# The tail of a block-transform 7x7 convolution: 128-column matrices, another split of the last evictions and of the last writes

## The chip, the cores and the metric

The kernel runs on one core of one Trainium2 chip. The metric is device time in microseconds of one execution. Five engines work side by side, each with its own queue of instructions: TensorE (PE; its weight loads are shown as PEld), VectorE (DVE), ScalarE (ACT), GpSimd (POOL) and SyncE (SP), which only issues DMAs and waits. DMAs may be issued from SP, POOL or ACT.

## The reference

A circular convolution of a 224 x 224 x 96 image with 7 x 7 x 96 x 96 weights, written as a product of two-dimensional real Fourier transforms:

```python
def reference(x, w):
    B, H, W, C = x.shape          # 1, 224, 224, 96
    K = w.shape[0]                # 7
    wp = jnp.pad(w, ((0, H - K), (0, W - K), (0, 0), (0, 0)))
    Xf = rfft2(x.astype(float32), axes=(1, 2))
    Wf = rfft2(wp.astype(float32), axes=(0, 1))
    Yf = jnp.einsum('bhwi,hwio->bhwo', Xf, Wf)
    return irfft2(Yf, s=(H, W), axes=(1, 2)).astype(bfloat16)
```

Image, weights and result are bfloat16.

## The kernel before

The image's rows are cut into NJ = 8 blocks of B = 28 rows, each with 6 rows of overlap, and every block is carried along the rows into a short real transform of length 32 (plus two extra points), 17 "slots" of two real parts each. Along the columns there is no transform: seven taps, with even and odd pixels treated apart. The columns are handled in NT = 7 tiles of 32 pixels. For each tile and slot, `b_round` does the tap products on TensorE (stationary: the transformed pixels, 128 columns; moving: 96 transformed weights of `WF`), and VectorE and GpSimd make the sums into `yf`. For tiles 0 to 5 the sums are written to a scratch tensor in DRAM, read back in another layout (`tt`) and turned into output rows with the matrix `G` (`c_jobs`), while the next tile's tap products run.

The last tile, TL = 6, does not go through DRAM. Its sums stay in SBUF (`YA` for the first SA = 13 slots, `YB` for the other four), VectorE transposes them in 32 x 32 blocks into `TA` and `TB` (`turn_a`, `turn_b`), and the inverse transform uses other matrices, `GY`: one for `TA` (`GA`) and four for `TB` (`GB`). `GY` is built on GpSimd by five copies from `GX`, which small DMAs fill from `G` (`g_parts`, L661 to L672), during the middle tiles; `GX` is set to zero first (L824). Each matrix has 4 * B = 112 columns, one for each of the 28 rows in each of 4 column quarters.

The tail is the code from L879 on. After `turn_b` and the remaining `c_jobs`, 16 units (j, h) are worked off, j the block of rows and h the half of the pixels:

- `first(j, h)` takes a PSUM bank and does one matmul with `GA`, 384 moving elements.
- `second(j, h, ...)` adds four matmuls with `GB`, 96 moving elements each, and then calls `tail_evac`, which copies the bank to SBUF as bfloat16.
- Eight firsts run ahead. The seconds follow in order, and from the fifth second to the twelfth each is followed by one more first (8 banks of PSUM, LF = 4), so first number 8 + n needs the bank of eviction n.
- After each odd unit, both halves of block j are in `yo`, and one DMA writes 28 rows x 4 quarters x 768 elements to the output (168 KB).

`tail_evac` counts calls in `tail[0]`, which is set to 2 just before, and gives odd counts to VectorE and even ones to ScalarE. The writes go by block: even j from SP (`DE`), odd j from GpSimd (`GE`), the last, j = 7, from ScalarE (`SE`). Instructions of one engine are held in program order by the `_Ordered` wrapper, so all instructions carry L86 in the profile, the line of its helper, and are told apart by their tiles. `evac`, the function for evictions before the tail, shares them out by a running estimate of load, and passes them to `tail_evac` when `tail[0]` is not zero.

Of the kernel before, what the change touches and what calls it, by code (L numbers as in the profile page):

```python
# [8 lines left out]
BF16 = mybir.dt.bfloat16  # L9
# [5 lines left out]
B = 28  # L15
# [5 lines left out]
NJ = 8  # L21
# [13 lines left out]
SA = 13  # L35
NB4 = 4
YMAX = 3
YBUF = 4
JGB = ((0, 3), (3, 6), (6, 9), (9, 12), (12, 15), (15, 17))
LAG = 4  # L40
# [13 lines left out]
def kernel(  # L54
# [38 lines left out]
    VE, SE, GE, TE, DE = (_Ordered(e) for e in (nc.vector, nc.scalar, nc.gpsimd, nc.tensor, nc.sync))  # L93
# [9 lines left out]
    def bank():  # L103
        return pools["psb"].tile([128, 512], F32, name="pb")

    load = {"v": 0.0, "a": 0.0}
    tail = [0]
# [7 lines left out]
        return r  # L115

    def evac(out_ap, in_ap, n):
        if tail[0]:
            return tail_evac(out_ap, in_ap, n)
        cv, ca = 180 + 1.0 * n, 160 + 0.85 * n  # L120
        if load["v"] + cv <= load["a"] + ca:
            load["v"] += cv
            return VE.tensor_copy(out=out_ap, in_=in_ap)
        load["a"] += ca
        return SE.copy(out=out_ap, in_=in_ap)

    def tail_evac(out_ap, in_ap, n):
        tail[0] += 1
        return VE.tensor_copy(out=out_ap, in_=in_ap) if tail[0] % 2 else SE.copy(out=out_ap, in_=in_ap)

    def dma(out_ap, in_ap):
        return DE.dma_start(out=out_ap, in_=in_ap)
# [258 lines left out]
    def new_xf(t, s0=0, s1=NS):  # L391
        xf = xf_bufs[t % 2]
        xf_tiles[t] = xf
        if t > 0:
            prev = xf_tiles[t - 1]
            for ph in range(2):
                o, i = (v[0:C, ph, :, s0:s1, p:p + HALO, :].rearrange("c r s w j -> c r s (w j)") for v, p in ((xf, 0), (prev, TW)))
                apart(("A", t), ("halo", s0), SE.copy(out=o, in_=i))
                load["a"] += 160 + 0.85 * 2 * (s1 - s0) * HALO * NJ
        return xf  # L400
# [34 lines left out]
    def then_load(f, t, jg):  # L435
        def g():
            f()
            if t < NT:
                load_x(t, jg)
        return g  # L440
# [11 lines left out]
    def f_jobs(t, part):  # L452
        s0, s1 = SH2[part], SH2[part + 1]
        n = 2 * (s1 - s0) * JG
        nr = -(-TW * n // 512)
        e = [-(-TW * i // nr) for i in range(nr + 1)]
        fv = Fm[:, :, s0:s1].rearrange("p r s j -> p r (s j)")

        def mk_(jg, a, b, ph):
            def f():  # L460
                pa = bank()
                for k in range(b - a):
                    i = 2 * (a + k) + ph
                    TE.matmul(pa[:, k * n:(k + 1) * n], lhsT=xbuf(t, jg)[:, i * C:i * C + 128], rhs=fv, start=True, stop=True)
                xo = xf_tiles[t][0:C, ph, :, s0:s1, HALO + a:HALO + b, jg * JG:(jg + 1) * JG]
                pi = pa[0:C, 0:(b - a) * n].rearrange("c (w r s j) -> c r s w j", r=2, s=s1 - s0, w=b - a)
                return apart(("A", t), (a, jg, ph, part), evac(xo, pi, (b - a) * n))
            return f
        return [[mk_(jg, a, b, ph) for a, b in zip(e[:-1], e[1:]) for ph in range(2)] for jg in range(2)]
# [40 lines left out]
    def b_round(t, s, mid, end, ydve=False, planes=()):  # L510
# [11 lines left out]
        else:  # L522
            for (y0, y1) in YGRP:
                if s == y0:
                    yf_cur[t] = (yf_pool.tile([128, YMAX, 2, 2, C], BF16, name="yf"), y0, y1)
            yf, y0, y1 = yf_cur[t]
# [134 lines left out]
    def g_parts():  # L661
        for q in range(4):
            dma(GX[q * SR:q * SR + 2 * SA, 0, q * B:q * B + B], G[0:2 * SA, 0:B])
            yield
        for q in range(4):
            for b in range(NB4):
                r = q * SR + b * SRB
                dma(GX[r:r + SRB, 1 + b, q * B:q * B + B], G[2 * SA:2 * NS, 0:B])
                yield
        for k in range(NB4 + 1):  # L670
            GE.tensor_copy(out=GY[:, k].rearrange("p (m q) -> p q m", q=4), in_=GX[:, k].rearrange("p (q m) -> p q m", q=4))
            yield  # L672

    yo_free = [J_bufs[2][0:4 * B, i * PXC * C:(i + 1) * PXC * C] for i in range(2)]
# [58 lines left out]
    def queue_c(t):  # L733
        pend.extend((t, *k) for k in LT)
        pump()
# [20 lines left out]
    stmp_cm.__exit__(None, None, None)  # L756
    yf_pool = ctx.enter_context(tc.tile_pool(name="yf", bufs=YBUF))
    tv_pool = ctx.enter_context(tc.tile_pool(name="tv", bufs=2))
# [12 lines left out]
    def fills(qs, k):  # L771
        def f():
            for q in qs:
                pace(q, k)
        return f
# [3 lines left out]
    def add(a, b, jobs):  # L779
        qs.append([a, b, jobs, len(jobs)])  # L780
# [14 lines left out]
    for r in range(NS + LAG):  # L795
        if r == 0:
            add(0, 4, fj[1][1] + fj[2][1])
        for p in range(3):
            if r == (1, 3, 5)[p]:
                new_xf(1, SH2[p], SH2[p + 1])  # L800
                fj = f_jobs(1, p)
                if p == 2:
                    for jg in range(2):
                        fj[jg][-1] = then_load(fj[jg][-1], 2, jg)
                add(2 * r + 1, 2 * r + (5, 5, 4)[p], fj[0] + fj[1])
        for p in range(3):
            if r == SH2[p + 1] + 1 - (p == 2):
                new_xf(2, SH2[p], SH2[p + 1])
                fj = f_jobs(2, p)
                if p == 2:  # L810
                    for jg in range(2):
                        fj[jg][-1] = then_load(fj[jg][-1], 3, jg)
                add(2 * r, 2 * r + (8, 7, 5)[p], fj[0] + fj[1])
        if r == PGRP[-2][1] + 1:
            assert not any(q[2] for q in qs[:len(PGRP) - 1])
            wtmp_cm.__exit__(None, None, None)
            t_pool = ctx.enter_context(tc.tile_pool(name="tt", bufs=NTT, side="right"))
            t2_pool = ctx.enter_context(tc.tile_pool(name="tt2", bufs=1, side="right"))
            yo_pool = ctx.enter_context(tc.tile_pool(name="yo", bufs=2, side="right"))
            g_pool = ctx.enter_context(tc.tile_pool(name="gp", bufs=1, side="right"))  # L820
            GX = g_pool.tile([128, 1 + NB4, 4 * B], BF16, name="GX")
            GY = g_pool.tile([128, 1 + NB4, 4 * B], BF16, name="GY")
            GA, GB = GY[:, 0], GY[:, 1:]
            GE.memset(GX[:], 0.0)  # L824
        if r == NS + 3:
            queue_c(0)
        for t in range(2):
            s = r - LAG * t
            if not 0 <= s < NS:
                continue  # L830
            now = bursts.pop((r, t), ())
            now = jit(*now) if now else ()
            both = LAG <= r < NS
            b_round(t, s, fills(qs, 2 * r + (t if both else 0)), fills(qs, 2 * r + (t if both else 1)), False, now)
    assert not bursts and nburst == 2 * len(JGB)
    if NP2:
# [3 lines left out]
        pools["ps"], pools["psb"] = (c.__enter__() for c in ps_cms)  # L840
    cj = c_jobs(0)
    gp = g_parts()
    for t in range(2, NT):
        if t == TL:
# [35 lines left out]
    load["v"] = 2 * BIAS + load["a"]  # L880
    for f in cj:
        f()
    tail[0] = 2
    assert not pend
    if NP2:
        for c in reversed(ps_cms):
# [2 lines left out]
    NC = 2 * 2 * C  # L889
    MO = 4 * B  # L890

    def first(j, h):
        pc = bank()[0:MO, 0:NC]
        TE.matmul(pc.rearrange("p (w g e) -> p w g e", w=2, e=4), lhsT=GA, rhs=TA[:, 2 * h:2 * h + 2, j], start=True, stop=False)
        return pc

    def second(j, h, pc, yo):
        po = pc.rearrange("p (w g b e) -> p b w g e", w=2, b=NB4, e=4)
        for b in range(NB4):
            TE.matmul(po[:, b], lhsT=GB[:, b], rhs=TB[:, 2 * h:2 * h + 2, j], start=False, stop=b == NB4 - 1)  # L900
        tail_evac(yo[0:MO, (j % 2) * 2 * NC + h * NC:(j % 2) * 2 * NC + (h + 1) * NC], pc, NC)
    order = [(j, h) for j in range(NJ) for h in range(2)]
    warm(WARM0)
    live = {k: first(*k) for k in order[:8]}
    LF = 4
    for i, (j, h) in enumerate(order):
        if i % 4 == 0:
            yo = t_pool.tile([128, TW // 2, 2 * C], BF16, name="tt").rearrange("p w e -> p (w e)")
        second(j, h, live[(j, h)], yo)
        k = i + 8 - LF  # L910
        if 8 <= k < len(order):
            live[order[k]] = first(*order[k])
        if i % 2 == 1:
            w0 = TL * 2 * TW
            eng = SE if j == NJ - 1 else GE if j % 2 else DE
            eng.dma_start(out=out[0, j * B:(j + 1) * B, w0:w0 + 2 * TW, :].rearrange("m (q w) c -> m q (w c)", q=4), in_=yo[0:MO, (j % 2) * 2 * NC:(j % 2 + 1) * 2 * NC])
    if not NP2:
        ps0_cm.__exit__(None, None, None)
# [30 lines left out]
```

## Time and profile before

| what | us |
|---|---|
| time, median of 3 runs | 265.87 (265.08 to 266.10) |
| the profiled execution, time | 266.41 |
| its span, first to last instruction | 264.7 |
| granted TensorE clock, mean | 0.993 |
| tail: 16 firsts and 64 seconds on TensorE | 252.78 to 259.04 |
| tail: evictions, VectorE | 8 of 0.55 each |
| tail: evictions, ScalarE | 8 of 0.48 each |
| tail: writes from SP, POOL, ACT | 4, 3, 1 |

The page gives busy times of each engine and, in its part 4, the chain of work that ended last, followed back from the end. The timeline lists instructions by start; adjacent ones of one engine and one kind are merged into a row with a count. "SPq" and "ACTq" are the engines' queues issuing a DMA; the duration there is that of issuing, not of the transfer. In rows by form, two numbers after the bar are busy microseconds and the mean of one in nanoseconds, and after the second bar stands the idle time before them with what ended it. The last columns of a row of windows are the granted clock, the DMA engines' busy share and GB/s. Times in all views count from the first instruction.

### The profile page before, as it was taken

How to read it: one execution, taken by the hardware profiler on the slowest of the kernel's cores; microseconds unless marked ns; L12 is line 12 of the kernel's file. 1: busy time of each engine (PE TensorE's matmuls, PEld its weight loads, DVE VectorE, ACT ScalarE, POOL GpSimd, SP SyncE). 2: the span in 40 equal slices, each digit the busy share in tenths (PEclk: the TensorE clock that was granted, in tenths of full speed). 3: DMA queues.
4: the chain of work that ended last, by engine and by line, in shares of the span. 5: the costliest groups of instructions: out<-in, count | busy, mean ns of one | idle time of the engine just before them, and what ended most of it. 6: DMA issues, size and time to landing. Idle time of an engine off the chain costs nothing.

```text
span 264.7 us, 12207 instructions
## 1 busy us (share of the span) xinstructions
PE 252.5 (95%) x5160; PEld 234.3 (89%) x5160; DVE 215.8 (82%) x459; ACT 198.6 (75%) x500; POOL 101.5 (38%) x166
## 2 busy tenths in 40 slices
PE   8799998999999999999999999999999999999981
PEld 3569898999999999998999998999999999999861
DVE  5729799898978979977888788777978889899981
ACT  5529997659795566898988869989798886666652
POOL 7781033345355553234123332543143222424420
PEclk9999999999999999999999999999999999999997
DMA  6766210451111299896979449597959753585135
GB/s 162 182 192 152 73 51 2 154 159 47 50 47 47 85 254 208 239 268 180 290 226 244 150 108 315 180 258 185 325 193 206 209 186 125 145 169 155 55 111 175
DMA packets 41416, 43.44 MB, mean 164 GB/s; under 512 B 30836, under 2 KB 33104, under 8 KB 41362
## 3 DMA queue, kind: packets, MB, share of 16 engines
q1 hardware_dynamic: 41044, 41.98, 56.6%
q8 instruction: 40, 0.66, 1.1%
q0 software_dynamic: 192, 0.52, 0.7%
q10 hardware_dynamic: 126, 0.17, 0.2%
q14 instruction: 14, 0.11, 0.1%
HBM read 22.09 MB, written 19.66 MB: 158 GB/s over the span
## 4 chain that ended last, share of the span: by engine, by line
PE 82%; ACT 5%; DVE 4%; issue 3%; DMA 3%; POOL 1%; SPq 1%; DVEq 0%; ACTq 0%
PE pb L86 82%; ACT WF L86 3%; DMA WF<-in_x_dram 3%; DVE WF L86 1%; ACT xf L86 1%; POOL yf L86 1%; DVE J L86 1%; DVE u L86 1%; DVE xf L86 1%; SPq L86 1%; DVE yf L86 0%; ACT tt L86 0%; DVE v L86 0%; ACT tt__676 L86 0%; ACT tt__2951 L86 0%
## 5 line engine op out<-in xcount | busy, mean ns | idle before, releaser
L86 PE MATMUL pb<-WF,J 96*128 96x96 bf16 x2821 | 162.6, 206 | 0.5 <-DVE WF L86 0.3
L86 PEld LDWEIGHTS <-J 96*128 96x128 bf16 x2821 | 137.9, 98 | 8.7 <-DVE u L86 1.5
L86 POOL TENSOR_TENSOR yf<-v,u 128x384 bf16<-128x384 f32 x70 | 69.1, 1001 | 129.5 <-issue 69.2
L86 ACT CAST xf<-pb 96x408 bf16<-96x408 f32 (+3 forms) x143 | 67.2, 487 | 10.3 <-PE pb L86 8.5
L86 PE MATMUL pb<-WF,xf 96*128 96x96 bf16 x952 | 60.2, 206 | 1.1 <-ACT xf L86 0.5
L86 DVE TENSOR_TENSOR J<-xf 96x1824 bf16<-96x1824 bf16 (+1 forms) x84 | 57.5, 724 | 0.1
L86 PEld LDWEIGHTS <-xf 96*128 96x128 bf16 x952 | 47.3, 98 | 1.9 <-issue 0.9
L86 PE MATMUL pb<-Fm,xn 118*128 118x136 bf16 (+3 forms) x640 | 45.5, 199 | 0.9 <-DVE u L86 0.8
L86 ACT CAST WF<-pb 96x480 bf16<-96x480 f32 (+1 forms) x59 | 29.0, 573 | 5.0 <-PE pb L86 5.0
L86 PE MATMUL pb<-tt,Gm 102*84 102x384 bf16 (+1 forms) x132 | 32.1, 326 | 0.0
L86 PEld LDWEIGHTS <-xn 118*128 118x128 bf16 x640 | 30.5, 97 | 1.2 <-issue 1.2
L86 ACT CAST yo<-pb 84x384 bf16<-84x384 f32 (+1 forms) x66 | 28.2, 484 | 2.9 <-PE pb L86 2.6
L86 ACT CAST J<-pb 84x384 bf16<-84x384 f32 (+1 forms) x65 | 28.0, 484 | 2.8 <-PE pb L86 2.8
L86 DVE TENSOR_TENSOR J<-J 96x912 bf16<-96x912 bf16 (+2 forms) x42 | 22.8, 542 | 0.0
L86 PE MATMUL pb<-wq 98*128 98x120 bf16 (+1 forms) x288 | 21.2, 225 | 0.0
L86 PEld LDWEIGHTS <-wq 98*128 98x128 bf16 x288 | 19.4, 148 | 0.2
L86 PE MATMUL pb<-wu 128*128 128x512 bf16 x43 | 11.8, 435 | 1.1 <-DVE ct L86 1.1
L86 DVE TENSOR_TENSOR yf<-v,u 128x384 bf16<-128x384 f32 x20 | 11.3, 567 | 0.7
L86 PEld LDWEIGHTS <-Gm 102*84 102x84 bf16 (+1 forms) x132 | 11.1, 117 | 0.8
L86 DVE CAST WF<-pb 96x480 bf16<-96x480 f32 (+1 forms) x13 | 7.5, 610 | 5.4 <-PE pb L86 5.2
L86 POOL TENSOR_TENSOR xn<-v,u 128x384 bf16<-128x384 f32 x8 | 7.2, 926 | 11.8 <-DVE v L86 11.8
L86 ACT COPY xf<-xf 96x816 bf16<-96x816 bf16 (+3 forms) x20 | 11.2, 621 | 0.0
(404 smaller groups left out, 254.3 us busy)
## 6 DMA issues: line engine op xcount, KB each, us to landing
scr<-yf SPq DMA_DIRECT2D x30, 288.0 KB
xn<-in_x_dram SPq DMA_DIRECT2D x12, 672.0 KB
tt<-scr SPq DMA_DIRECT2D x24, 336.0 KB
out_dram<-yo SPq DMA_DIRECT2D x12, 252.0 KB
out_dram<-J SPq DMA_DIRECT2D x12, 252.0 KB
tt<-scr SPq DMA_DIRECT2D x6, 288.0 KB
WF<-in_x_dram SPq DMA_DIRECT2D x2, 672.0 KB
scr<-yf SPq DMA_DIRECT2D x6, 192.0 KB
```

What stands on the lines that cost most here:

```text
L86: r = fn(*a, **k)
```

## The change

Three edits in the tail. `GY` gets 128 columns for each matrix instead of 112, with zeros in the last 16, and the PSUM outputs of `first` and `second` have 128 rows, of which the first 112 are evicted. `tail_evac` counts from 0 and gives VectorE the seven calls of `TAILV`, ScalarE the other nine. Blocks 1 and 3 are written from GpSimd, all others from SP. The branch from `evac` to `tail_evac` goes away.

```diff
+TAILV = (1, 3, 5, 8, 10, 12, 14)
...
     def evac(out_ap, in_ap, n):
-        if tail[0]:
-            return tail_evac(out_ap, in_ap, n)
         cv, ca = 180 + 1.0 * n, 160 + 0.85 * n
...
     def tail_evac(out_ap, in_ap, n):
         tail[0] += 1
-        return VE.tensor_copy(out=out_ap, in_=in_ap) if tail[0] % 2 else SE.copy(out=out_ap, in_=in_ap)
+        return VE.tensor_copy(out=out_ap, in_=in_ap) if tail[0] in TAILV else SE.copy(out=out_ap, in_=in_ap)
...
-            GE.tensor_copy(out=GY[:, k].rearrange("p (m q) -> p q m", q=4), in_=GX[:, k].rearrange("p (q m) -> p q m", q=4))
+            GE.tensor_copy(out=GY[:, k, 0:4 * B].rearrange("p (m q) -> p q m", q=4), in_=GX[:, k].rearrange("p (q m) -> p q m", q=4))
...
-            GY = g_pool.tile([128, 1 + NB4, 4 * B], BF16, name="GY")
+            GY = g_pool.tile([128, 1 + NB4, 128], BF16, name="GY")
             GA, GB = GY[:, 0], GY[:, 1:]
             GE.memset(GX[:], 0.0)
+            GE.memset(GY[:, :, 4 * B:], 0.0)
...
-    tail[0] = 2
+    tail[0] = 0
...
-        pc = bank()[0:MO, 0:NC]
+        pc = bank()[:, 0:NC]
...
-        tail_evac(yo[0:MO, (j % 2) * 2 * NC + h * NC:(j % 2) * 2 * NC + (h + 1) * NC], pc, NC)
+        tail_evac(yo[0:MO, (j % 2) * 2 * NC + h * NC:(j % 2) * 2 * NC + (h + 1) * NC], pc[0:MO], NC)
...
-            eng = SE if j == NJ - 1 else GE if j % 2 else DE
+            eng = GE if j in (1, 3) else DE
```

Numbered from 0, the evictions go V A V A V A V A V A V A V A V A before and V A V A V A A V A V A V A V A A after.

## The prediction

> **What bounds the kernel now.** I read the page first, then the chain of waits over the last 25 us, then the timeline of the tail engine by engine, and last the windows of DMA traffic.
>
> ```profile
> span 264.7 us, 12207 instructions
> PE 252.5 (95%) x5160; PEld 234.3 (89%) x5160; DVE 215.8 (82%) x459; ACT 198.6 (75%) x500; POOL 101.5 (38%) x166
> ...
> PE 82%; ACT 5%; DVE 4%; issue 3%; DMA 3%; POOL 1%; SPq 1%; DVEq 0%; ACTq 0%
> ```
>
> TensorE sets the time of the whole, but the edit leaves everything before the tail as it was, so the page's shares say nothing about it. The chain of waits shows where the tail begins and what it hangs on:
>
> ```profile
> 252.78 1.49 PE pb L86 x8
> 254.27 0.00 issue
> 254.27 4.36 PE pb L86 x64
> 258.64 0.02 issue
> 258.66 0.89 ACT tt L86 x2
> ```
>
> The eight first matmuls start at 252.78, the seconds at 254.27 (when VectorE's last transpose is done), and the last eviction ends at 259.55. The span ends at 264.70, so the last 5.15 us hold no compute at all: they are the last writes, their landing and the end of the program. The timeline, asked for one engine and narrow windows at a time, gives the eight writes (SP the j = 0, 2, 4, 6 ones, POOL j = 1, 3, 5, ACT j = 7):
>
> ```profile
> 255.38 0.93 SPq L86 DMA_DIRECT2D out_dram<-tt  x1
> 256.42 0.88 SPq L86 DMA_DIRECT2D out_dram<-tt  x1
> 257.85 0.80 SPq L86 DMA_DIRECT2D out_dram<-tt  x1
> 259.16 0.80 SPq L86 DMA_DIRECT2D out_dram<-tt  x1
> 258.88 0.59 POOL L86 DMA_DIRECT2D out_dram<-tt  x1 [0.87 <-ACT tt L86]
> 259.58 1.44 ACTq L86 DMA_DIRECT2D out_dram<-tt  x1
> ```
>
> One issue of this shape holds SP for 0.80 to 0.93 us. By the trace's semaphore events SP's four writes land at 258.19, 260.03, 261.49 and 263.47, that is 2.81, 3.61, 3.64 and 4.31 us after the issue began; POOL's at 259.74, 261.18 and 262.55; ACT's at 263.67, 4.09 us after its issue began. The last 1.03 us (263.67 to 264.70) are SP's remaining waits and the closing barrier. So the end is set by the last landing, and that by when the last two writes are issued and how long they take. The windows of DMA traffic show the room that is left:
>
> ```profile
> 260.00:261.00 1.00, 0.00 (x0) 0.00 (x0) 0.00 (x0) 0.00 (x0) 0.00 (x0) 1.00 0.80 249
> 262.00:263.00 1.00, 0.00 (x0) 0.00 (x0) 0.00 (x0) 0.00 (x0) 0.00 (x0) 0.50 0.60 214
> 263.00:264.00 1.00, 0.00 (x0) 0.00 (x0) 0.00 (x0) 0.00 (x0) 0.00 (x0) 0.50 0.01 2
> ```
>
> The last two columns are the DMA engines' busy share and GB/s: about 0.8 in most of 257 to 262 (0.81 in 257:258, 0.77 in 261:262), then it runs dry.
>
> **Matrices of 128 columns.** The rows that give the price:
>
> ```profile
> 254.27 1.19 PE L86 MATMUL pb<-xf,GY 128*112 128x96 bf16 x20
> 248.33 1.06 PE L86 MATMUL pb<-WF,J 96*128 96x96 bf16 x21
> L86 PEld LDWEIGHTS <-GY 128*112 128x112 bf16 x80 | 5.4, 131 | 2.3 <-POOL xf L86 1.5 <-issue 0.2
> L86 PEld LDWEIGHTS <-J 96*128 96x128 bf16 x2821 | 137.9, 98 | 8.7 <-DVE u L86 1.5 <-issue 0.9
> ```
>
> Twenty seconds of 112 columns take 1.19 us, of which the last one's own duration is 0.21: a pitch of (1.19 - 0.21)/19 = 51.5 ns. Twenty-one matmuls of the same 96 moving elements with 128-column matrices have (1.06 - 0.21)/20 = 42.6 ns, and their loads take 98 ns instead of 131. So 64 seconds x 8.9 ns = 0.57 us less TensorE. The 16 firsts move 384 elements at a pitch of 164 ns, set by the moving side, and keep it. The Trainium skill ("TensorE: Matmul & The Clock Gate", section "LDWEIGHTS (loading the stationary operand)") speaks against this: a load costs its column count over 1.2, so 107 ns for 128 against 93 for 112. The rows here stand the other way round, 98 against 131, and they decide; scaled by that rule the pitch would be an estimated 59 ns and TensorE 0.47 us later.
>
> The zeros behind the matrix cost POOL one memset of 80 columns, between the 0.125 us of a 32-column one and the 0.555 us of GX's 560. It follows GX's (87.19 to 87.75), and POOL is idle there until 89.20: covered; without that cover at most 0.56 us. The five copies into GY and the evictions' 112 rows do not change. The branch taken out of evac was never taken before the tail and evac is not called in it: nothing.
>
> **Evictions.** One takes VectorE 0.556 us and ScalarE 0.479; back to back they start 0.47 and 0.41 apart (starts at 255.145 and 255.610; 258.658 and 259.072), 0.04 after their last matmul ends. I walked all 16 through. The ring of eight banks now binds once: first number 8 waits for eviction 0 (ends 255.21, TensorE follows 0.055 later), and starts at 255.26 instead of 255.13. From there a first and four seconds take 164 + 4 x 42.7 = 335 ns instead of 370. Evictions 8 and 9 (ScalarE, VectorE; write j = 4) end at 257.29 and 257.70, 10 and 11 at 257.96 and 258.37, 12 and 13 at 258.63 and 258.88. The last matmul ends at about 258.62 instead of 259.04, but 12, 14 and 15 are all ScalarE's: 258.15, 258.56, 258.98, the last ending at 259.46 against 259.55. Of the 0.57 us, 0.09 is left here.
>
> **The writes.** Issue and landing are what remains. POOL keeps j = 1 and 3, a few hundredths earlier. SP issues j = 0 at 255.33, j = 2 at 256.37, j = 4 when eviction 9 is done, 257.79 (0.09 after a VectorE end, through two waits). Then SP is the queue that all wait in: j = 5, 6, 7 are ready at 258.46, 258.97 and 259.49, but each issue takes 0.80 and the step to the next 0.12 (256.305 to 256.423): 258.71, 259.63, 260.55. So the last write starts its issue 0.97 us later than ACT's did at 259.58. Behind it nothing waits but the end of the program. ACT's 1.44 us issue and POOL's third, with its landing at 262.55, go away; neither frees anything that is needed later.
>
> From issue to landing the bounds are 2.81 us (j = 0, alone on the DMA engines) and 4.31 us (j = 6, with POOL's and ACT's writes beside it). By 261.2 POOL's two writes have landed, as before. What is left then comes from one queue at a pitch of 0.92 us, and j = 0's packets took 0.91 us (256.95 to 257.85): each write is nearly alone, so I take 2.81. Sum: 260.55 + 2.81 = 263.36, against 263.67; plus the same 1.03 = 264.39, 0.31 less than the span.
>
> The profiled execution took 266.41 us, 1.71 around its span and 0.54 above the median of 265.87. 266.41 - 0.31 = 266.10; on the median, 265.56. About 1.33 us (0.5%) is what a measurement of this kernel can tell from no change; its three runs span 265.08 to 266.10.
>
> **Rivals.**
>
> *SP's issues slow down behind one another (slower).* For it: ACT's issue, made while SP's last was in flight, took 1.44 us, and after a row of loads SP's own issues grow:
>
> ```profile
> 229.58 0.58 SPq L86 DMA_DIRECT2D tt<-scr  x1
> 231.41 1.65 SPq L86 DMA_DIRECT2D tt<-scr  x1
> 233.10 2.14 SPq L86 DMA_DIRECT2D tt<-scr  x1
> ```
>
> With 1.44 for j = 5, 6 and 7 they start at 258.71, 260.27 and 261.83, the last issue ends at 263.27, lands 1.88 after (2.81 - 0.93) at 265.15, span 266.18, +1.48: 267.35. The span is 261.86 plus three issues, so it ties the old at 0.95 each and passes +0.5% at 1.39. Against it: j = 2 followed j = 0 by 0.12 and took 0.88. Chance 0.12.
>
> *The last write lands as slowly as SP's last one did, 4.31 us.* 260.55 + 4.31 + 1.03 = 265.89, +1.19: 267.06. For it: j = 5 to 7 share one queue. Against: that 4.31 had three queues at 0.8 busy. Chance 0.10.
>
> *Issue time does not count (faster).* If j = 5 to 7 were issued as soon as ready, as plain rows are in 0.32 us (write of yo at 252.92, landed 2.48 later), j = 7 would start at 259.54 and land at 262.02: span 263.05, -1.65: 264.22. The Trainium skill ("DMA: Bandwidth & Descriptors", section "Issuing engines are not separate DMA queues") says so: issuing from several engines saves only the sequencer's time, usually small beside the DMA. The four rows of 0.80 to 0.93 out of 2.8 to 4.3 us speak against it. Chance 0.10.
>
> *The change does not do what it says: the matrices load no faster.* Eviction 9 then ends at 257.90 instead of 257.70, j = 4 to 7 all start 0.2 later, span 264.6, -0.1: 265.8. The page's 98 ns are against it, though wq's 128-column loads, strided, took 148. Chance 0.08.
>
> **How the numbers follow.** The forecast has 0.60. Faster by over 0.5%: 0.10 for the issue rival and 0.08 for the low end of the forecast, whose spread is that of the runs: 0.18. Slower: 0.12. Within 0.5%: 0.70. The range reaches down to the issue rival, 264.2, and up to the slow landing, 267.1; what is outside is the slow-issue rival and little else.
>
> **What would show it.** Loads of GY near 98 ns and seconds at a pitch near 43: the first step. The last ScalarE eviction ending near 259.5: the second. SP's last three issues 0.9 apart with the last at 260.5 to 260.6: the third; at 1.2 and more the slow-issue rival; near 259.5 the fast one. A landing 2.8 after the last issue, DMA running dry before 263: the fourth. A time under 264.5 or over 267.2 makes the prediction wrong, and so does a change anywhere before 252 us.

## The result and the profile after

The changed kernel takes 264.69 us (median of 18 runs) against 265.37 for the kernel before in the same comparison: a ratio of 0.9977, 95% interval 0.9969 to 0.9985, so 0.6 us less, within the 0.5% that was called "no change". The forecast was 0.31 less and its range 264.2 to 267.1. (Its 265.56 started from 265.87, the median of three runs; the 18 runs give 265.37.)

The page of the changed kernel, first lines (its execution took 264.65 us):

```profile
span 263.0 us, 12207 instructions
PE 252.0 (96%) x5160; PEld 233.3 (89%) x5160; DVE 215.1 (82%) x458; ACT 198.7 (76%) x501; POOL 101.3 (39%) x166
```

The two spans differ by 1.75 us, and most of that arises long before the tail. The chain of waits of the changed kernel has the tail 1.38 us earlier than before (firsts at 251.40, not 252.78):

```profile
251.40 1.46 PE pb L87 x8
252.87 0.03 issue
252.89 3.83 PE pb L87 x60
256.73 0.02 issue
256.75 0.86 ACT tt L87 x2
```

The timeline shows where that comes from. The first tap product starts at 22.00 before and at 20.68 after; from there to the first second the two traces take 232.28 and 232.22. First row: before; second: after.

```profile
22.00 0.51 PE L86 MATMUL pb<-WF,xf 96*128 96x96 bf16 x8 [0.46 <-ACT xf L86]
```

```profile
20.68 0.51 PE L87 MATMUL pb<-WF,xf 96*128 96x96 bf16 x8 [0.46 <-ACT xf L87]
```

So, from here on, the tail is measured from the start of the first second (the 96-element matmul on `GY`) to the end of the span: 264.70 - 254.27 = 10.43 before, 262.95 - 252.89 = 10.06 after. That difference, 0.37, is what the forecast's sum of 0.31 is to be held against. Times called "relative" below count from that first second.

The timeline of SP in the changed kernel, its six issues, each asked for in a window of its own:

```profile
253.94 0.93 SPq L87 DMA_DIRECT2D out_dram<-tt  x1
254.98 0.87 SPq L87 DMA_DIRECT2D out_dram<-tt  x1
256.37 0.80 SPq L87 DMA_DIRECT2D out_dram<-tt  x1
257.28 0.80 SPq L87 DMA_DIRECT2D out_dram<-tt  x1
258.19 0.80 SPq L87 DMA_DIRECT2D out_dram<-tt  x1
259.09 0.80 SPq L87 DMA_DIRECT2D out_dram<-tt  x1
```

From the third on they are 0.91 apart, with nothing between them: SP is the pace. By the semaphore events the last write lands at 261.99, 2.91 after its issue began, where ACT's had needed 4.09 and SP's last 4.31. The windows of DMA traffic (last columns: clock, DMA share, GB/s) show the DMA engines at 0.73 to 0.83 up to the end and then empty at once:

```profile
258.60:259.60 1.00, 0.00 (x0) 0.00 (x0) 0.00 (x0) 0.00 (x0) 0.00 (x0) 1.00 0.73 226
259.60:260.60 1.00, 0.00 (x0) 0.00 (x0) 0.00 (x0) 0.00 (x0) 0.00 (x0) 1.00 0.83 263
260.60:261.60 1.00, 0.00 (x0) 0.00 (x0) 0.00 (x0) 0.00 (x0) 0.00 (x0) 0.65 0.76 255
261.60:262.60 1.00, 0.00 (x0) 0.00 (x0) 0.00 (x0) 0.00 (x0) 0.00 (x0) 0.50 0.00 2
```

The weight loads and the pitch, answering to the rows shown for 112 columns:

```profile
252.89 1.02 PE L87 MATMUL pb<-xf,GY 128*128 128x96 bf16 x20
L87 PEld LDWEIGHTS <-GY 128*128 128x128 bf16 x80 | 4.4, 96 | 2.9 <-POOL xf L87 1.5 <-issue 0.3
```

(1.02 - 0.20)/19 = 43 ns instead of 51.5, and 96 ns for a load instead of 131.

### The profile page after: what moved, and what is told of

The parts are those of the page before. It is cut to its first block, busy times and chain, and to the rows that moved or that the text cites. A ratio compares the mean times of both kernels' runs of the same rounds, so it can differ in the third digit from the quotient of the medians.

```text
span 263.0 us, 12207 instructions
## 1 busy us (share of the span) xinstructions
PE 252.0 (96%) x5160; PEld 233.3 (89%) x5160; DVE 215.1 (82%) x458; ACT 198.7 (76%) x501; POOL 101.3 (39%) x166
## 4 chain that ended last, share of the span: by engine, by line
PE 79%; POOL 7%; DVE 4%; issue 4%; ACT 3%; ACTq 0%; POOLq 0%; DVEq 0%
PE pb L87 79%; POOL ct L87 6%; ACT WF L87 2%; DVE WF L87 1%; DVE u L87 1%; POOL yf L87 1%; DVE J L87 1%; DVE xf L87 1%; ACT xf L87 1%; DVE v L87 0%; DVE yf L87 0%; ACT tt L87 0%; ACT tt__676 L87 0%; ACTq L944 0%; ACT ct L87 0%
## 5 line engine op out<-in xcount | busy, mean ns | idle before, releaser
L87 ACT COPY xf<-xf 96x816 bf16<-96x816 bf16 (+3 forms) x20 | 11.2, 624 | 0.0
```

The costliest lines, as they stand in the source:

```text
L87: r = fn(*a, **k)
```

## The experiments

**One part at a time.** Four kernels: the columns alone, the split alone, the owners of the writes alone, and the whole change with the last write back on ScalarE's queue.

The columns alone are the kernel before with the edits to `GY`, `first` and `second` (two of the lines):

```diff
+            GY = g_pool.tile([128, 1 + NB4, 128], BF16, name="GY")
...
+        pc = bank()[:, 0:NC]
```

> The kernel before with the 128-column matrices alone (evictions alternate, the writes stay with SP, POOL and ACT). Tail here means from the start of the first second (the first 96-element matmul on GY) to the end of the span: 10.43 us before, 10.06 with the whole change. Theory (the end is the last issue plus a landing of a fixed length): seconds at a pitch of 43 ns, last eviction 0.34 earlier, SP's j = 6 and ACT's j = 7 issued 0.33 earlier, so a tail of 10.1. Rival (the writes are bound by the DMA engines, not by when they are issued): the tail stays within 0.1 of 10.43. Second question, the start-up: the first tap product starts at 22.00 in the profile before and at 20.68 after. If this is chance, the runs here scatter over both; if it comes from ScalarE's queue being used for a DMA, they stay with the kernel before (about 0.3 to 0.4 us above the changed kernel beyond the tail); if it comes from GY's larger tile, they go with the changed kernel.

Measured: ratio 0.9999 (0.9986 to 1.0012), tail 10.79. ACT's j = 7 is issued 0.35 earlier, at 4.96 relative instead of 5.31, as the theory had it, and lands 4.81 after that instead of 4.09. The rival named for it comes nearer, and even it expected too little: in this profile the landing took back more than the earlier issue won, and the time is that of the kernel before. The start-up is at 20.70.

The split alone:

```diff
-        return VE.tensor_copy(out=out_ap, in_=in_ap) if tail[0] % 2 else SE.copy(out=out_ap, in_=in_ap)
+        return VE.tensor_copy(out=out_ap, in_=in_ap) if tail[0] in TAILV else SE.copy(out=out_ap, in_=in_ap)
```

> The kernel before with the split of seven and nine evictions alone. Theory: with TensorE's old pace three ScalarE evictions (12, 14, 15) end the tail, the last ending 0.21 later than before, and j = 4, 6 and 7 are issued 0.14 to 0.21 later: tail 10.6, time +0.2. Rival (DMA-bound tail): tail within 0.1 of 10.43. Start-up: as before if ScalarE's queue or GY's tile decides it.

Measured: 1.0017 (1.0006 to 1.0029), tail 11.01. The issues are later by about what was expected (ACT's at 5.48, 0.17 later), and the landing is again longer, 4.50. The split alone costs time.

The writes alone:

```diff
-            eng = SE if j == NJ - 1 else GE if j % 2 else DE
+            eng = GE if j in (1, 3) else DE
```

> The kernel before with the new owners of the writes alone (POOL j = 1 and 3, SP the rest, none by ACT). Theory: SP issues j = 4 at the old time, j = 5, 6 and 7 each 0.92 later, the last at 2.76 after j = 4, landing 2.9 behind: tail 10.3, time -0.2 from the tail. Start-up: if ScalarE's queue decides it, the first tap product starts near 20.7 and the time falls by a further 0.3 to 0.4; if GY's tile decides it, it stays as before; if it is chance, the runs scatter over both.

Measured: 0.9980 (0.9971 to 0.9989), tail 10.18. The last issue is at 6.30, 1.0 later than ACT's was before, and lands 2.92 after. Nearly the whole gain of the change is in this one line. Its time is within the interval of the changed kernel's.

The whole change with j = 7 on ScalarE's queue:

```diff
-            eng = GE if j in (1, 3) else DE
+            eng = SE if j == NJ - 1 else GE if j in (1, 3) else DE
```

> The changed kernel with the last write, j = 7, back on ScalarE's queue. Theory: ACT issues it right after its last eviction, 1.07 earlier than SP did, for 1.44 us, and SP's last is j = 6, 0.9 before the old last: the tail falls to between 9.45 and 9.9 (10.06 with the whole change), depending on how much the two queues slow each other's landings. Start-up: if ScalarE's queue decides it, the time rises again by 0.3 to 0.4 against the changed kernel beyond the tail; otherwise it stays.

Measured: 0.9982 (0.9962 to 1.0003), tail 10.49. The timeline of this kernel has both last writes under way at once, SP's j = 6 and ACT's j = 7:

```profile
258.21 0.80 SPq L87 DMA_DIRECT2D out_dram<-tt  x1
258.04 1.44 ACTq L87 DMA_DIRECT2D out_dram<-tt  x1
```

They land 4.17 and 4.16 after their issues began. Both issues began 0.9 to 1.1 earlier than the changed kernel's last one (5.12 and 5.29 relative against 6.20), and the end is 0.43 later. The theory as written there, an issue plus a landing of known length, falls for two queues at the end. The 0.43 is one profile against another, and by the interval the time cannot be told from the changed kernel's; but ten of the eleven runs, 265.08 to 265.76 us, are above the slowest of the eleven that the writes alone took in the same comparison (264.67 to 265.00).

On the start-up: the first tap product is at 20.62 to 20.70 in all four, with ScalarE's queue in use and without, with the wider tile and without. Neither decides it.

**What sets the pace: issues or bytes.** Three kernels on the changed one: three writes by POOL, none by POOL, a quarter of the bytes left out; and, on the kernel before, the padded tile without its use.

```diff
-            eng = GE if j in (1, 3) else DE
+            eng = GE if j in (1, 3, 5) else DE
```

> The changed kernel with j = 5 written by POOL again, so three writes by POOL and five by SP, the last, j = 7, still SP's. Theory of the prediction (SP's issues, 0.92 apart, set when the last write starts; it lands 2.8 to 2.9 later): j = 7 is issued 0.6 earlier and the tail (from the first second's start to the end of the span, 10.06 with the change) falls to 9.45. Rival (the DMA engines are full, and more than one queue at the end slows the last landing): the last write waits behind POOL's, and the tail stays at 10.0 or grows.

Measured: 1.0002 (0.9986 to 1.0019), tail 10.62: all of the change's gain is gone. SP's last issue is 0.66 earlier (5.54 relative) and lands 4.05 after. The windows of this kernel, aligned with those of the changed one (both start 5.71 relative):

```profile
258.80:259.80 1.00, 0.00 (x0) 0.00 (x0) 0.00 (x0) 0.00 (x0) 0.00 (x0) 1.00 0.79 241
259.80:260.80 1.00, 0.00 (x0) 0.00 (x0) 0.00 (x0) 0.00 (x0) 0.00 (x0) 1.00 0.83 250
260.80:261.80 1.00, 0.00 (x0) 0.00 (x0) 0.00 (x0) 0.00 (x0) 0.00 (x0) 0.55 0.60 203
261.80:262.80 1.00, 0.00 (x0) 0.00 (x0) 0.00 (x0) 0.00 (x0) 0.00 (x0) 0.50 0.09 32
```

The writes start earlier, but the traffic thins out (0.60, then 0.09) where the changed kernel is still at 0.76 and then done. The packets' summed time is the same, 72.9 us against 72.6 over all DMA engines: no more work, but a ragged end to it.

All eight by SP (`eng = DE`):

> The changed kernel with all eight writes issued by SP. Theory: eight issues 0.91 apart from 1.05 after the first second's start, the last at 7.45 instead of 6.20, landing 2.8 later: tail 11.2, time +1.2. Rival (DMA-bound): the same bytes from one queue, tail 10.1 or less.

Measured: 1.0027 (1.0013 to 1.0040), tail 11.33. The eight landings take 2.75 to 2.82 each, and the last issue is at 7.62. The windows are flat, at 0.7 of the engines:

```profile
259.55:260.55 1.00, 0.00 (x0) 0.00 (x0) 0.00 (x0) 0.00 (x0) 0.00 (x0) 0.53 0.69 189
260.55:261.55 1.00, 0.00 (x0) 0.00 (x0) 0.00 (x0) 0.00 (x0) 0.00 (x0) 0.50 0.70 197
```

The theory said 11.2, the rival 10.1 or less. With one queue the issues set the end, at 172,032 bytes each 0.91 us, and the DMA engines, at 0.7 where POOL's help brought them to 0.83, are not full.

POOL's two writes left out:

```diff
-            eng = GE if j in (1, 3) else DE
...
-            eng.dma_start(...)
+            if j not in (1, 3):
+             DE.dma_start(...)
```

> The changed kernel without POOL's two writes: blocks 1 and 3 of the last tile are not written, a quarter of the tail's bytes, while SP's six issues stay where they are. Theory: j = 7 is issued at the same 6.2 and lands 2.8 later: tail 9.95, time -0.1. Rival (DMA-bound): a quarter less to move at some 0.6 us for each write, tail 8.9, time -1.2.

Measured: 0.9975 (0.9960 to 0.9989), tail 9.88. The last issue is at 6.19, its landing 2.77. A quarter of the bytes is worth 0.18 us at most (a kernel below that writes everything has the same 9.88): the theory's 9.95, not the rival's 8.9. So in the changed kernel POOL's two early writes ride along nearly for nothing.

The padded tile, with the matmuls left at 112 columns (the tile, the copies and the memset are those of the change; the line that differs from it):

```diff
-            GA, GB = GY[:, 0], GY[:, 1:]
+            GA, GB = GY[:, 0, 0:4 * B], GY[:, 1:, 0:4 * B]
```

> The kernel before with GY's tile padded to 128 columns and the zeros written, but with only 112 columns used by the matmuls: the memset and the new addresses without anything else. Theory: nothing, a time within 0.2 us of the kernel before, loads of GY at 131 ns; and a second look at the tail of the kernel before, 10.4 in its profile, where the kernel with the columns alone showed 10.8. If GY's tile shortens the start-up, the time falls by 0.3.

Measured: 0.9993 (0.9980 to 1.0006), tail 10.35, start-up at 20.70. The memset and the new addresses cost and bring nothing that these runs can tell. The tail of this profile nevertheless starts late, at 254.24: TensorE stops once for 1.07 us, at 122.04, with no wait that the profile shows. So a single execution can be delayed outside the tail, which is why tails and not whole spans of single profiles are compared here.

**What the split is worth in company, and a better mix.** Columns and writes, evictions alternating:

```diff
-        return VE.tensor_copy(out=out_ap, in_=in_ap) if tail[0] in TAILV else SE.copy(out=out_ap, in_=in_ap)
+        return VE.tensor_copy(out=out_ap, in_=in_ap) if tail[0] % 2 else SE.copy(out=out_ap, in_=in_ap)
```

> The 128-column matrices and the new owners of the writes, with the evictions alternating as before. What has shown itself so far: with SP alone at the end the writes start 0.91 apart and land 2.8 to 2.9 after their issue. By that, eviction 9 is ScalarE's and ends at about 3.35 after the first second's start, j = 4 is issued at 3.4, j = 7 at 6.15: tail 10.0, the same as with the whole change within 0.1, so the split of seven and nine is worth nothing. Rival: the split is needed, tail 10.3 or more.

Measured: 264.63 us, 0.9969 (0.9955 to 0.9983), tail 9.88: j = 4 is issued at 3.36 (3.48 in the changed kernel), the last write at 6.08, landing 2.83. The split is not needed; this is the shortest tail that writes everything, though its time cannot be told from the changed kernel's.

POOL writing j = 1, 2 and 4:

```diff
-            eng = GE if j in (1, 3) else DE
+            eng = GE if j in (1, 2, 4) else DE
```

> The changed kernel with POOL writing j = 1, 2 and 4 and SP the other five. Theory of the prediction (SP's issues alone): j = 3 is issued at 2.85, j = 5 at 4.2, j = 7 at 6.0, tail 9.85. By what the run with j = 5 on POOL showed (a write of POOL's that is still moving when SP's last ones are makes these land 4.0 to 4.5 after their issue): POOL's j = 4 is issued at about 4.1 and lands near 8, SP's j = 6 and 7 land late, tail 10.3 to 10.6.

Measured: 0.9978 (0.9964 to 0.9992), tail 10.20. SP's last issue is 0.25 earlier (5.95) and lands 3.22 after. POOL's third write has landed at 7.66 relative, earlier than expected, and costs less than j = 5 did. Against the changed kernel it saves nothing: 0.25 won by the issue, 0.31 lost by the landing, too small a difference for one profile of each. In one and the same comparison the columns and writes took 264.63 us and this kernel 264.97.

**How steady is the old ending?** The kernel before twice more, for its profile.

> The kernel before, unchanged, for another profile. The two profiles of this ending so far have tails of 10.43 and 10.35 and a delay of about 1.3 us elsewhere each. Theory: 10.4 again, and the part of the measured 0.61 us that the tail does not explain lies ahead of it. Rival: with three queues at the end the landing scatters, and here it is 10.7 to 10.8, as in the kernel with the columns alone.

> The kernel before once more, a second draw of the same: 10.4 by the theory, anywhere from 10.3 to 10.9 by the rival.

Measured: tails of 10.20 and 10.66. The four profiles of this ending (with the one on record and the padded tile) are 10.43, 10.35, 10.20 and 10.66, mean 10.41. Identical issues, to 0.03 us, but landings of ACT's write between 3.86 and 4.32: the scatter is in the landing. The rival's scatter is there, then, though around the theory's 10.4.

All tails side by side, each from one profile; "issue" is the start of the issue of the write that landed last, relative to the first second, and the remaining 1.0 us is the end of the program:

| kernel | last writes by | issue | landing | tail |
|---|---|---|---|---|
| before (and again, twice) | POOL, SP, ACT | 5.31 | 4.09 (3.86, 4.32) | 10.43 (10.20, 10.66) |
| columns alone | POOL, SP, ACT | 4.96 | 4.81 | 10.79 |
| split alone | POOL, SP, ACT | 5.48 | 4.50 | 11.01 |
| before, padded tile | POOL, SP, ACT | 5.31 | 4.01 | 10.35 |
| change, j = 7 by ACT | SP, ACT | 5.29 | 4.17 | 10.49 |
| change, j = 5 by POOL | POOL, SP | 5.54 | 4.05 | 10.62 |
| change, POOL j = 1, 2, 4 | SP | 5.95 | 3.22 | 10.20 |
| writes alone | SP | 6.30 | 2.92 | 10.18 |
| the change | SP | 6.20 | 2.91 | 10.06 |
| columns and writes | SP | 6.08 | 2.83 | 9.88 |
| change without POOL's writes | SP | 6.19 | 2.77 | 9.88 |
| change, all by SP | SP | 7.62 | 2.76 | 11.33 |

## Why the prediction was right, and where it was not

**Columns.** The pitch and the loads came as worked out: 43 ns (42.7 used) and 96 ns. A load of 128 columns takes less time here than one of 112 (96 against 131 ns), so the rule by column count that was weighed there does not hold between the two.

**Evictions.** First number 8 did wait for its bank, at 0.98 relative (forecast 0.99); the last matmul ended at 4.33 (4.35), the last ScalarE eviction at 5.09 (5.19).

**The writes.** SP's j = 4 was issued at 3.48 (forecast 3.52), 0.07 after eviction 9 ended (0.09), j = 7 at 6.20 (6.28), 0.91 apart (0.92); the landing took 2.91 (2.81), the end of the program 0.97 (1.03). Sum: 10.06 against 10.12. Taking the landing of a write that is nearly alone was the choice that decided the forecast, and the run without POOL's writes (2.77) and that with all by SP (2.75 to 2.82) show it was the right row. Only the last write came that near to being alone: SP's j = 4, 5 and 6 landed 3.83, 3.61 and 3.24 after their issues, while POOL's second write, which landed at 6.99, and what had queued up beside it ran out.

**The sentence that failed** is that ACT's issue and POOL's third write "go away; neither frees anything that is needed later". They freed the DMA engines for the end. The sentence is also at odds with the sum itself, which takes 2.81 for the last landing instead of 4.09 because the last write is alone, and it is alone only because those two are gone. Read as a pace of issues alone, the sum would have said that whatever issues the last write sooner ends sooner. Three kernels did so (columns alone, j = 7 by ACT, j = 5 by POOL), and each ended 0.4 to 0.7 later than the change. With two or three queues at the end the last landing takes 3.9 to 4.8 us, with one 2.8 to 2.9, and in each of these kernels that difference is more than the earlier issue won (j = 5 by POOL: 0.66 won, 1.14 lost). POOL's j = 1, 2 and 4 lies between, with 3.22, and is no clear case. The four profiles of the old ending scatter by 0.46 among themselves, but every ending with two or three queues (10.20 to 11.01) is above every ending in which SP is alone with its last writes and takes six of the eight (9.88 to 10.18). The change gains because its last writes come from one queue, although they are issued 0.9 us later.

**The parts.** The forecast follows one path, through SP's issue of j = 4, and never prices the split of the evictions by itself. The runs do. With the writes in place, j = 4 is issued at 3.57 relative with nothing else changed, at 3.36 with the columns and at 3.48 with columns and split: the columns bring 0.21 there, and the split takes 0.12 of it back. The last issue follows (6.30, 6.08, 6.20), and the tails go the same way (10.18, 9.88, 10.06), with differences that one profile of each cannot secure. Measured alone in time, the columns gained nothing, the split lost 0.17%, the owners of the writes gained 0.20%, against 0.23% for the whole change.

**The rivals.** SP's issues did not slow down behind one another: from the third on they take 0.80 each, in the run with eight of them too. The landing of 4.31 did not come; in the runs here, landings that long belong to several queues. "Issue time does not count" is refuted: j = 7 was ready at 5.09, when its last eviction ended, and its issue started only at 6.20; and with all eight on SP the tail grew by 1.27. By the Trainium skill ("DMA: Bandwidth & Descriptors", section "Issuing engines are not separate DMA queues"), DMAs from several engines run on the same DMA engines and interleave, and issuing from several saves only the sequencer's time, usually small beside the DMA. The first agrees with these runs: SP's writes land 2.75 to 2.82 after their issue with all eight on SP, 3.6 to 3.8 beside POOL's in the changed kernel. The second does not hold for this shape: issuing takes 0.80 of the 2.8 from issue to landing.

**The size.** Measured is 0.6 us (0.68 between the medians), twice the forecast, and the tails give 0.35 of it (10.41, the mean of four profiles, against 10.06). The rest lies ahead of the first tap product, of which the forecast says nothing. It starts at 22.00, 20.98 and 20.95 in the three profiles of the kernel before, at 20.59 to 20.78 in those of the other kernels. The execution with 22.00 took 266.41 us, more than any of the 18 in the comparison. Without it the parts add up: 20.97 to the first tap product, 232.28 from there to the first second and 10.41 of tail make 263.66 before; 20.68, 232.22 and 10.06 make 262.96 after. That is 0.70 apart, 0.29 of it in the start-up.

The earlier start does not belong to one of the edits: the kernels with the columns alone, the split alone, the writes alone and the padded tile alone all have it (20.62 to 20.70). The loads of image and weights land at other times there, though the same lines issue them. Why is open: all three profiles of the kernel before lie above all eleven others, which does not look like chance, but no run separates a cause. The forecast had named a change anywhere before 252 us as a sign against itself. There is one, so its sum is borne out for the tail alone, and the other half of the gain is no merit of the forecast. (It gave 264.2 as the low end of its range and 264.5 as the time below which it would be wrong; 264.69 is above both.)

## What to carry to other kernels

When a kernel ends in a row of writes, look at the landing of the last one and not only at its issue: a write that shares the DMA engines with another queue may land a microsecond and more later than one that follows its like in a single queue. Here it paid to give early writes to the other queue, to let it run out, and to end on one queue whose pace the DMA engines could follow. A part that is worth half a microsecond on its engine is worth nothing until the wait behind it is the one that ends last; try parts alone and in company.

## What the runs showed of the hardware that was not expected

- The cost of several queues at the end is not in work: the packets of the tail take 71 to 75 us summed over the engines in the kernels where POOL has a part (78 with all by SP, 59 without POOL's writes), while the last packet ends between 8.58 relative (columns and writes) and 9.49 (split alone). By the semaphore events, a write of SP's or ACT's lands in 14 pieces (behind a first event at 1.2 to 1.5 us). Those of the last write come 2.61 to 2.91 after its issue in the changed kernel, but 2.69 to 4.05 with j = 5 by POOL, and 3.41 to 4.17 with j = 7 by ACT. So beside POOL's queue some pieces come late, and beside ACT's all of them do. Which of the engines end late the records here do not say.
- One issue of 28 x 4 pieces of 1536 bytes holds SP for 0.80 us (0.93 and 0.88 for the first two) where a plain write of 84 rows of 3072 bytes holds it for 0.32, so this shape alone limits SP's queue to 172,032 bytes per 0.91 us, 189 GB/s; the traffic in the run with all by SP is just that, 189 to 197 GB/s.
